# Gates of the first two chunks: from two groups of one to one group worked in parts

## The chip, the cores and the metric

The kernel runs on one core of one Trainium2 chip. The time is device microseconds of one execution; the time of a kernel is the median of its runs. Below, PE is the matrix engine (PEld its weight loads), DVE the vector engine, ACT the scalar engine, POOL the GpSimd engine and SP the SyncE queue that issues most transfers.

## What is computed

A gated linear recurrence with a complex gate, and behind it a mixer over its output. All is float32.

```python
# batch 4, heads 8, seq 768, head_dim 48
mag = sqrt(a_re**2 + a_im**2)
scale = minimum(mag, 0.999) / (mag + 1e-06)
ar, ai = a_re * scale, a_im * scale
for t in range(seq):                       # per batch and head, state is 48 x 48 complex
    S_re, S_im = ar*S_re - ai*S_im + outer(k[t], v[t]), ar*S_im + ai*S_re
    y[t] = q[t] @ S_re
x = y as (batch, seq, heads*head_dim)      # 4 x 768 x 384
u = x + (x.T @ U @ V).T                    # mixes positions through rank 32
out = u + relu(u @ w_ch1) @ w_ch2          # 384 -> 1536 -> 384
```

## The kernel before, in words

**Tiles.** The 768 positions of each of 4 batches are cut into chunks of 128, 24 chunks in all; a chunk is a tile of 128 positions by 384 (8 heads of 48). The recurrence is not run step by step. The gate of each position is written as a size and an angle, the logarithms and the angles are summed over the chunk by matmuls with triangular matrices, and q and k are weighted with exponentials and rotations made from the sums, so that what is left of a chunk is matmuls.

**Gates.** `gates(g)` (lines 531 to 653) makes these for a group of chunks (`GROUPS`, line 237). Before, the groups are chunk 0 alone, chunk 1 alone, and then pairs. `magnitudes` (547) takes a_re and a_im through Square, Ln, Exp, Relu and Sign on ACT and some additions on DVE into l, the logarithm of the size; `within` (571) sums l by one matmul ("es ps", line 575) and takes two exponentials, es. `totals` (580) has the matmuls "tot" (601), one exponential E, and transfers of E into a tile T (588). `turns` (608) takes Arctan, then the product z (DVE L611) and a scaling ("fourth", ACT), and `angles` (617) sums z by the matmul "ph" (632), to which a chunk that isn't the first of its batch adds the last row of the chunk before by "tail" (635), and rounds the sum (F, DVE L638). `waves` (641) takes Abs and two Sines into cs. The functions Ln and Exp stand in one table of ACT and Arctan and Sin in another; `switch` (322) loads a table, and the plan keeps every function that needs one between the loads that belong to it. So each group costs two loads.

**Chunks.** `prep` (661) multiplies q and k by es, then by cs into QKC, of which there is one buffer, and transposes the product on PE ("tr", line 682) into QK. `chain` (690) has the products "inner" (716) and "corners" (766), the multiplications of QK by T between them (DVE L329), and the state: "ks ps", "dk", "y".

**Mixer.** `mixer(m)` (856) works on two chunks: "mixed", "uTp", then "up" (916) with w1, Relu, then "down" with w2 (1062 for the first mixer, 1105 for others; the last mixers use fewer products, "few", 974). Its products have the lowest urgency, so they fill PE where chunks leave it free. The weights arrive as 64-bit numbers: `single` (463) loads a piece into one of two raw buffers (SP, 768 KB), converts it by six DVE operations (486 to 496), and adds a remainder by a POOL transfer (499).

**Order.** Nothing is issued in the order of the text. Each operation is given to `Plan` (45) with an engine, a cost, a rank and what it reads and writes. `order` (80) then walks through time and gives each free engine the ready operation with the smallest urgency; the urgencies are a table by kind and number (26). Where PE would stand idle before the first mixer product, the plan writes a filler: a matmul "spare" of no use (1232). After the first mixer product it writes none. The plan also reckons with the arrival of PE's program in blocks (`fetch`, 262: first 95, then every 127 records, asked for 16 ahead, 3.7 us).

The driver (1196 to 1225) says which gates are made known before which chunks:

```python
    for g in range(NG):
        load_a(g)
        magnitudes, totals, turns, waves = gates(g)
        rank = "gates", GROUPS[g][0]
        switch(rank, exps)
        ...
        magnitudes()
        if g:
            totals()
        else:
            later = [totals]
        switch(rank, trigs)
        turns()
```

## Time and profile before

| | us |
|---|---|
| median of 3 runs (704.29 to 705.83) | 705.47 |
| the profiled execution | 704.41 |
| its span, first to last instruction | 702.6 |
| PE busy / DVE busy / ACT busy / POOL busy | 681.1 / 540.1 / 418.1 / 51.8 |
| fillers on PE (line 1232), 219 of them | 61.4 |
| mean granted clock of PE | 0.990 |

The span leaves out 1.8 us around the instructions. A float32 matmul is two records on PE in most of its uses, so the 219 fillers are 438 records in the profile; transposes are one record. Busy times are sums of durations; on PE neighbouring matmuls overlap, so the pace is read from starts. In the part on costly groups, the name in front of the arrow is the tile that is written. In the answer on waits the columns are the sum, the number and the longest of the waits; "issue" means that nothing that the profile records was waited for.

The first stage goes to 152.24 us, where the first up matmul starts. In it, chunks 0 to 5 are prepared and w1 and part of w2 are converted.

### The profile page before, as it was taken

The numbers are of one execution on the slowest core, as the hardware profiler recorded it, in microseconds if no ns is written. First come the engines' busy times: TensorE is split into PE (matmuls) and PEld (weight loads), VectorE is DVE, ScalarE is ACT, GpSimd is POOL, SyncE is SP. The second block draws the span as 40 slices with busy tenths as digits, with TensorE's granted clock in tenths as the row PEclk, the third lists the DMA queues.
The fourth block names the chain that finished last, engine by engine and source line by source line (L and its number), as shares of the span: only waits on it lengthen the run. The fifth ranks groups of instructions, "written<-read, shape, count | busy, mean of one in ns | idle before, by whom it ended". The sixth has DMA issues, their size and how long they took to land.

```text
span 702.6 us, 27047 instructions
## 1 busy us (share of the span) xinstructions
PE 681.1 (97%) x12148; PEld 601.0 (86%) x12148; DVE 540.1 (77%) x877; ACT 418.1 (60%) x778; POOL 51.8 (7%) x92
## 2 busy tenths in 40 slices
PE   7989998999999999999999999999999999999998
PEld 6877877877688888879888888889999999899997
DVE  5899998888898887759678487879887787455734
ACT  6786987678797687977784953651624415041230
POOL 5110000011000010001000000000000000000000
PEclk9999999799999999999999999999999999999999
DMA  7876855498424343252334032040121000000000
GB/s 185 172 184 149 186 103 141 91 209 176 99 51 90 68 94 76 41 109 53 63 77 93 9 67 59 10 98 26 23 42 35 14 27 17 18 7 24 7 18 22
DMA packets 165267, 53.24 MB, mean 76 GB/s; under 512 B 154080, under 2 KB 160416, under 8 KB 165152
## 3 DMA queue, kind: packets, MB, share of 16 engines
q1 hardware_dynamic: 161072, 42.26, 27.7%
q0 software_dynamic: 4080, 9.27, 5.6%
q8 instruction: 95, 1.56, 0.9%
q14 instruction: 20, 0.16, 0.1%
HBM read 33.59 MB, written 4.72 MB: 55 GB/s over the span
## 4 chain that ended last, share of the span: by engine, by line
PE 79%; ACT 9%; DVE 7%; issue 3%; DMA 1%; SPq 0%; DVEq 0%; ACTq 0%
PE down L1105 21%; PE few L974 12%; PE up L916 12%; PE inner L716 6%; PE tr L682 5%; ACT gate L326 3%; PE dk L802 3%; PE y L841 3%; PE spare L1232 2%; PE ks ps L787 2%; PE down L1062 2%; PE es ps L575 2%; PE ph L632 2%; PE tot L601 2%; PE y L833 2%
## 5 line engine op out<-in xcount | busy, mean ns | idle before, releaser
L329 DVE TENSOR_TENSOR QK<-QK,T 112x1024 f32<-112x1024 f32 x120 | 145.8, 1221 | 6.5 <-PE corners L766 5.3
L916 PE MATMUL up<-uT,w 128*128 128x256 f32 x432 | 98.7, 381 | 0.0
L916 PEld LDWEIGHTS up<-uT,w 128*128 128x128 f32 x432 | 80.7, 190 | 12.0 <-DVE uT L906 0.2
L326 ACT ACTIVATE gate<-gate 128x768 f32<-128x768 f32 (+1 forms) x91 | 71.0, 792 | 6.2 <-DVE gate L611 2.0
L1105 PE MATMUL down<-w,h 128*128 128x192 f32 x396 | 73.2, 330 | 0.0
L982 ACT COPY h<-few 128x512 f32<-128x512 f32 x36 | 20.8, 584 | 85.2 <-PE few L974 85.1
L685 ACT COPY QK<-tr 112x512 f32<-112x512 f32 x96 | 52.0, 588 | 32.6 <-PE tr L682 32.3
L1105 PEld LDWEIGHTS down<-w,h 128*128 128x128 f32 x396 | 63.9, 190 | 2.7 <-issue 1.3
L1232 PE MATMUL spare<-ident 128*128 128x128 f32 x438 | 61.4, 289 | 2.1 <-POOL ident masks.py:199 1.5
L332 DVE TENSOR_TENSOR h<-few,h 128x512 f32<-128x512 f32 x54 | 37.2, 691 | 30.2 <-PE few L974 26.2
L1232 PEld LDWEIGHTS spare<-ident 128*128 128x128 f32 x438 | 55.1, 198 | 5.9 <-issue 1.9
L716 PEld LDWEIGHTS inner<-QK 112*32 112x32 f32 x4608 | 45.9, 110 | 16.4 <-issue 10.7
L716 PE MATMUL inner<-QK 112*32 112x16 f32 (+1 forms) x4608 | 51.2, 190 | 4.9 <-issue 4.5
L682 PE MATMUL tr<-ident,QKC 128*112 128x128 f32 x384 | 51.9, 275 | 1.2 <-ACT QK L685 0.8
L329 DVE TENSOR_TENSOR QKC<-qk,cs 128x768 f32<-128x768 f32 x48 | 45.9, 956 | 9.3 <-PE tr L682 6.6
L332 DVE TENSOR_TENSOR xo<-down,xo 128x192 f32<-128x192 f32 (+1 forms) x79 | 29.8, 388 | 27.0 <-PE down L1105 25.2
L682 PEld LDWEIGHTS tr<-ident,QKC 128*112 128x112 f32 x384 | 42.3, 133 | 6.1 <-ACT QK L685 1.8
L974 PE MATMUL few<-gate,w 128*128 128x128 f32 x336 | 43.1, 277 | 0.0
L1049 POOL DMA_DIRECT2D out_dram<-xo x32 | 17.9, 560 | 338.9 <-DVE xo L332 278.8
L850 ACT COPY xo<-y 64x192 f32<-64x192 f32 x96 | 30.1, 313 | 19.2 <-PE y L841 16.0
L722 DVE COPY_PREDICATED DG<-mask,inner 128x128 f32<-128x128 int32 (+1 forms) x72 | 24.6, 344 | 20.4 <-PE inner L716 20.3
L974 PEld LDWEIGHTS few<-gate,w 128*128 128x128 f32 x336 | 40.0, 192 | 0.3
(131 smaller groups left out, 1272.0 us busy)
## 6 DMA issues: line engine op xcount, KB each, us to landing
stage<-in_moe_w_ch_dram SPq DMA_DIRECT2D x12, 768.0 KB, 6.5
gate<-in_a_re_dram SPq DMA_DIRECT2D x24, 192.0 KB, 3.2
gate<-in_a_im_dram SPq DMA_DIRECT2D x24, 192.0 KB, 4.3
qk<-in_q_dram SPq DMA_DIRECT2D x24, 192.0 KB, 4.0
qk<-in_k_dram SPq DMA_DIRECT2D x24, 192.0 KB, 4.4
VP<-in_v_dram SPq DMA_DIRECT2D x24, 192.0 KB, 3.3
w<-stage POOLq DMA_DIRECT2D x12, 384.0 KB, 5.7
T<-E SPq DMA_DIRECT2D x44, 96.0 KB, 2.5
```

What stands on the lines that cost most here:

```text
L326: return nc.scalar.activation(out=o, in_=i, func=f, **kw)
L329: nc.vector.tensor_tensor(out=o, in0=a, in1=b, op=OP.mult)
L332: nc.vector.tensor_tensor(out=o, in0=a, in1=b, op=OP.add)
L682: nc.tensor.transpose(out=get(*ps)[0:DQ, j], in_=get(*qkc)[:, hh * HH + j].rearrange("p u d -> p (u d)")[:, 0:DQ], identity=ident)
L685: ACT(c_act(HH * CH) - 0.05, R1, lambda u=u, hh=hh, ps=ps: nc.scalar.copy(out=get(*QK)[:, u, hh * HH:(hh + 1) * HH], in_=get(*ps)[0:DQ]), ...
L716: nc.tensor.matmul(out=get(*ps)[js, h], lhsT=k_of(h)[:, js], rhs=part(q_of(h)[:, js], "p"), start=True, stop=True, tile_position=(0, j * BLK))
L722: nc.vector.copy_predicated(out=to, mask=part(mask[:, n], "p").unsqueeze(1).to_broadcast(list(to.shape)), data=a if hf < 8 else a.rearrang ...
L850: ACT(c_act(HH * D), RR, lambda r=r, u=u: nc.scalar.copy(out=get(*xi).rearrange("p (a u d) -> p a u d", u=2, d=D)[r * HC:(r + 1) * HC, :, ...
L916: nc.tensor.matmul(out=get(*ps)[:, e], lhsT=w1[:, f, (ff + e) * 128:(ff + e + 1) * 128], rhs=get(*uT)[:, f], start=(f == 0), stop=(f == KD ...
L974: nc.tensor.matmul(out=get(*ps)[:, q], lhsT=w()[:, q * 128:(q + 1) * 128], rhs=v[0](), start=(n == 0 and q == 0), stop=True, skip_group_ch ...
L1105: nc.tensor.matmul(out=get(*to)[:, part], lhsT=x(j), rhs=y[:, j], start=(first and j == 0), stop=(j == KH - 1), skip_group_check=not first)
L1232: nc.tensor.matmul(out=spare[0], lhsT=ident, rhs=ident, start=True, stop=True)
```

## The change

The first two chunks become one group. Within it, operations are still made for one chunk each (`PARTS`), so that chunk 0 doesn't wait for chunk 1 at every step, but both chunks stand between the same table loads: 12 groups instead of 13. `totals` of the first group isn't put off any more, and its transfers carry two chunks each. `PAIRED` and `AT_ONCE` count groups and are shifted by one, so that they mean the same chunks. The loads of a of chunks 0 and 1 are given ranks next to each other. A preparation waits for its own chunk's part of cs.

All urgencies are replaced by other numbers. This moves instructions on every engine through the whole kernel.

```diff
-    GROUPS = [(0, 1), (1, 2)] + [(n, n + GC) for n in range(2, NT, GC)]
+    GROUPS = [(n, n + GC) for n in range(0, NT, GC)]
+    PARTS = [[(n, n + 1) for n in range(GC)]] + [[g] for g in GROUPS[1:]]
...
-    PAIRED = 6
+    PAIRED = 5
...
-    AT_ONCE = (0, 1, 2, 3)
+    AT_ONCE = (0, 1, 2)
...
-                SP(c_dma(DM), ("load", (0, 0.5, 3)[g] if g < 3 else lo + 3), lambda nm=nm, src=src, i=i: nc.sync.dma_start(
+                SP(c_dma(DM), ("load", i / 20 if g == 0 else 3 if g == 1 else lo + 3), lambda nm=nm, src=src, i=i: nc.sync.dma_start(
...
         def magnitudes():
             ring(l, "GL", GL)
-            ACT(ca, R1, lambda: act(t(x), t(ar), AF.Square), [ar], [x])
+            for part in PARTS[g]:
+                magnitudes_of(*part)
+
+        def magnitudes_of(lo, hi):
+            t, R1, W = t_of(lo, hi), ("gates", lo), (hi - lo) * DM
+            ca, cd = c_act(W), c_dve(W)
+            X, Y, L, N = (b + (lo,) for b in (x, y, l, n))
+            AR, AI = ([b + (i,) for i in range(lo, hi)] for b in (ar, ai))
+            ACT(ca, R1, lambda: act(t(x), t(ar), AF.Square), AR, [X])
...
         def turns():
-
-            table(ca, R2, lambda: act(t(x), t(x), AF.Arctan), [], [x])
+            for part in PARTS[g]:
+                turns_of(*part)
...
         def waves():
-            cs = ("cs", g)
-            buffer(cs, "cs", 2, [128, GC, H, 2, D])
+            buffer(("cs", g), "cs", 2, [128, GC, H, 2, D])
+            for part in PARTS[g]:
+                waves_of(*part)
...
-                [qk, ("cs", g)], [qkc])
+                [qk] + [("cs", g, (w, part)) for w in range(2)], [qkc])
...
         magnitudes()
-        if g:
-            totals()
-        else:
-            later = [totals]
+        totals()
```

An excerpt of the urgencies:

```diff
-    "w2": {0: -111.09, 2: 522.21, 4: 896.97, 6: -52.37, 8: 604.14, 10: 640.8, 12: -317.28},
-    "gates": {0: -265.04, 1: 268.17, 2: 43.76, 4: -996.63, 6: 89.37, 8: 509.61, 10: -55.71, 12: 809.99, 14: -95.12,
-        16: 160.61, 18: -122.91, 20: -425.54, 22: -1729.17},
+    "w2": {0: -1266.56, 2: -21.8, 4: -981.82, 6: -74.99, 8: 354.48, 10: -1170.63, 12: 259.42},
+    "gates": {0: 253.11, 1: -1390.93, 2: -0.7, 4: -1280.16, 6: 565.76, 8: -1068.17, 10: -187.84, 12: -54.04, 14: 550.2,
+        16: 60.85, 18: -1317.29, 20: 219.78, 22: -1069.82},
```

More of the change, by code (lines that the diff above doesn't have):

```diff
@@ L26 @@
 URGENCY = {
-    "w1": {0: 577.09, 1: -1319.32, 2: 484.43, 3: -236.69, 4: 471.82, 5: -1058.73, 6: 187.51},
-    "w2": {0: -111.09, 2: 522.21, 4: 896.97, 6: -52.37, 8: 604.14, 10: 640.8, 12: -317.28},
-    "gates": {0: -265.04, 1: 268.17, 2: 43.76, 4: -996.63, 6: 89.37, 8: 509.61, 10: -55.71, 12: 809.99, 14: -95.12,
-        16: 160.61, 18: -122.91, 20: -425.54, 22: -1729.17},
-    "angles": {0: -126.72, 1: -84.17, 2: -1567.87, 4: -1150.68, 6: -325.13, 8: 105.31, 10: 61.73, 12: 732.88,
-        14: -1148.2, 16: 655.25, 18: 538.84, 20: -116.45, 22: 233.15},
@@ L33 @@
-    "prep": {0: -1639.87, 1: -367.99, 2: -1022.47, 3: -12.47, 4: -106.92, 5: -436, 6: -74.87, 7: 260.1, 8: -1682.29,
-        9: 278.7, 10: 47.08, 11: 569.46, 12: -1452.21, 13: -249.3, 14: -287.97, 15: -363.52, 16: -269.7,
-        17: -1664.43, 18: -240.93, 19: 153, 20: -1089.48, 21: -198.95, 22: -127.5, 23: 757.32},
-    "levels": {0: 731.75, 1: -318.03, 2: 17.02, 3: -430.68, 4: -436.08, 5: -170.38, 6: 221.56, 7: 124.72, 8: -1567.59,
-        9: -1453.16, 10: -1698.36, 11: -60.78, 12: 502.58, 13: 523.21, 14: -1475.59, 15: 515.81, 16: -1265.88,
-        17: 487.77, 18: -263.92, 19: 16.81, 20: 723.89, 21: -1759.83, 22: -1111.46, 23: -160.12},
@@ L39 @@
-    "rest": {0: 468.93, 1: -1086.12, 2: 24.25, 3: -218.54, 4: -1119.41, 5: -346.92, 6: 0.68, 7: -1700.8, 8: 681.55,
-        9: -376.72, 10: -229.72, 11: -305.85, 12: -1069.62, 13: 601.71, 14: -282.72, 15: 204.95, 16: 59.77,
-        17: 552.08, 18: -62.45, 19: 466.03, 20: -1105.96, 21: -351.77, 22: -1688.33, 23: 463.92},
+    "w1": {0: -1281.04, 1: -1220.88, 2: -1207.45, 3: 315.61, 4: 369.7, 5: 444.04, 6: 70.95},
+    "w2": {0: -1266.56, 2: -21.8, 4: -981.82, 6: -74.99, 8: 354.48, 10: -1170.63, 12: 259.42},
@@ new lines @@
+    "gates": {0: 253.11, 1: -1390.93, 2: -0.7, 4: -1280.16, 6: 565.76, 8: -1068.17, 10: -187.84, 12: -54.04, 14: 550.2,
+        16: 60.85, 18: -1317.29, 20: 219.78, 22: -1069.82},
+    "angles": {0: -1303.82, 1: -1298.68, 2: -1227.51, 4: 58.46, 6: 57.41, 8: -1315.3, 10: -1053.02, 12: 620.73,
+        14: 187.25, 16: -891.55, 18: 148.92, 20: -161.38, 22: -1298.55},
+    "prep": {0: -1294.88, 1: 125.6, 2: -26.13, 3: 96.73, 4: 102.92, 5: 146.86, 6: 553.65, 7: 283.9, 8: 120.02,
+        9: -991.17, 10: -32.91, 11: 113.94, 12: -202.96, 13: 14.8, 14: 318.58, 15: 357.43, 16: 269.94, 17: 521.08,
+        18: 158.53, 19: -163.04, 20: 127.47, 21: 184.1, 22: 205.57, 23: -1204.94},
@@ new lines @@
+    "levels": {0: 201.22, 1: 294.56, 2: -15.94, 3: 207.38, 4: -1236.01, 5: 275.3, 6: 572.46, 7: 14.34, 8: -1057.92,
+        9: 306.71, 10: 125.53, 11: 133.52, 12: 287.15, 13: 373.35, 14: 82.96, 15: 592.16, 16: 289.79,
+        17: -1204.78, 18: -1075.08, 19: 91.86, 20: 733.17, 21: -1309.23, 22: 119.93, 23: -1230.17},
+    "rest": {0: 93.55, 1: 47.27, 2: 273.41, 3: 257.67, 4: -1050.04, 5: -1068.08, 6: -1240.77, 7: -1208.87, 8: -1033.73,
+        9: -1290.81, 10: 34.85, 11: -1143.56, 12: -162.29, 13: -197.24, 14: -1046.5, 15: 612.4, 16: 244.97,
+        17: -1261.21, 18: 98.64, 19: -1031.75, 20: -1297.46, 21: 239.78, 22: 384.61, 23: 164.23},
@@ L531, in gates @@
     def gates(g):
-        lo, hi = GROUPS[g]
-        W = (hi - lo) * DM
-        R1, R2 = ("gates", lo), ("angles", lo)
-        ca, cd = c_act(W), c_dve(W)
         x, y, l, n, z, ar, ai = names = [(nm, g) for nm in ("x", "y", "l", "n", "z", "ar", "ai")]
-        def t(b):
-            a = get(*b)
-            return (a.rearrange("p c h d -> p (c h d)") if b[0][0] == "a" else a)[:, 0:W]
+        first = GROUPS[g][0]
         def of(b, i):
-            return get(*b)[:, (i - lo) * DM:(i - lo + 1) * DM]
+            return get(*b)[:, (i - first) * DM:(i - first + 1) * DM]
@@ L547, in magnitudes, with t_of, t @@
+        def t_of(lo, hi):
+            def t(b):
+                a = get(*b)
+                return (a.rearrange("p c h d -> p (c h d)") if b[0][0] == "a" else a)[:, (lo - first) * DM:(hi - first) * DM]
+            return t
         def magnitudes():
             ring(l, "GL", GL)
-            ACT(ca, R1, lambda: act(t(x), t(ar), AF.Square), [ar], [x])
-            ACT(ca, R1, lambda: act(t(y), t(ai), AF.Square), [ai], [y])
-            DVE(cd, R1, lambda: add(t(x), t(x), t(y)), [y], [x])
-            DVE(c_one(W), R1, lambda: nc.vector.tensor_scalar(out=t(x), in0=t(x), scalar1=M2LO, scalar2=M2HI, op0=OP.max,
-                                                              op1=OP.min), [], [x])
@@ L554, in magnitudes @@
-            ACT(ca, R1, lambda: act(t(n), t(ar), AF.Abs), [ar], [n])
-            table(ca, R1, lambda: act(t(l), t(x), AF.Ln), [x], [l])
-            table(ca, R1, lambda: act(t(x), t(l), AF.Exp, scale=0.5), [l], [x])
-            DVE(cd, R1, lambda: add(t(x), t(x), t(n)), [n], [x])
-            table(ca, R1, lambda: act(t(y), t(l), AF.Exp, scale=-0.5, bias=leps), [l], [y])
-            table(ca, R1, lambda: act(t(y), t(y), AF.Ln, bias=1.0), [], [y])
-            ACT(ca, R1, lambda: act(t(l), t(l), AF.Relu, scale=-0.5, bias=lmax), [], [l])
@@ L562, in magnitudes @@
-            DVE(cd, R1, lambda: nc.vector.scalar_tensor_tensor(out=t(l), in0=t(l), scalar=LNMAX, in1=t(y), op0=OP.subtract,
-                                                               op1=OP.add), [y], [l])
-            table(ca, R1, lambda: act(t(x), t(x), AF.Ln), [], [x])
-            table(ca, R1, lambda: act(t(x), t(x), AF.Exp, scale=-1.0), [], [x])
-            DVE(cd, R1, lambda: mul(t(x), t(x), t(ai)), [ai], [x])
-            ACT(ca, R1, lambda: act(t(n), t(ar), AF.Sign, bias=tiny), [ar], [n])
+            for part in PARTS[g]:
+                magnitudes_of(*part)
@@ new lines, in magnitudes_of @@
+        def magnitudes_of(lo, hi):
[4 more added lines that the diff above has]
+            ACT(ca, R1, lambda: act(t(x), t(ar), AF.Square), AR, [X])
+            ACT(ca, R1, lambda: act(t(y), t(ai), AF.Square), AI, [Y])
+            DVE(cd, R1, lambda: add(t(x), t(x), t(y)), [Y], [X])
+            DVE(c_one(W), R1, lambda: nc.vector.tensor_scalar(out=t(x), in0=t(x), scalar1=M2LO, scalar2=M2HI, op0=OP.max,
+                                                              op1=OP.min), [], [X])
+            ACT(ca, R1, lambda: act(t(n), t(ar), AF.Abs), AR, [N])
+            table(ca, R1, lambda: act(t(l), t(x), AF.Ln), [X], [L])
+            table(ca, R1, lambda: act(t(x), t(l), AF.Exp, scale=0.5), [L], [X])
+            DVE(cd, R1, lambda: add(t(x), t(x), t(n)), [N], [X])
+            table(ca, R1, lambda: act(t(y), t(l), AF.Exp, scale=-0.5, bias=leps), [L], [Y])
+            table(ca, R1, lambda: act(t(y), t(y), AF.Ln, bias=1.0), [], [Y])
+            ACT(ca, R1, lambda: act(t(l), t(l), AF.Relu, scale=-0.5, bias=lmax), [], [L])
+            DVE(cd, R1, lambda: nc.vector.scalar_tensor_tensor(out=t(l), in0=t(l), scalar=LNMAX, in1=t(y), op0=OP.subtract,
+                                                               op1=OP.add), [Y], [L])
+            table(ca, R1, lambda: act(t(x), t(x), AF.Ln), [], [X])
+            table(ca, R1, lambda: act(t(x), t(x), AF.Exp, scale=-1.0), [], [X])
+            DVE(cd, R1, lambda: mul(t(x), t(x), t(ai)), AI, [X])
+            ACT(ca, R1, lambda: act(t(n), t(ar), AF.Sign, bias=tiny), AR, [N])
@@ L568, in magnitudes, with within @@
             for i in range(lo, hi):
-                within(i)
-        def within(i):
+                within(i, R1, L)
+        def within(i, R1, L):
             ps, es = ("es ps", i), ("es", i)
@@ L575, in within @@
             PE(0.65, R1, lambda: nc.tensor.matmul(out=get(*ps), lhsT=mid, rhs=of(l, i), start=True, stop=True),
-               [l, ("mid", 0)], [ps, ("sums", g, i)], takes=[es], steps=2)
+               [L, ("mid", 0)], [ps, ("sums", g, i)], takes=[es], steps=2)
             for u in range(2):
@@ L583, in totals @@
             ring(tt, "T", TS)
-            for i in range(lo, hi):
-                of_blocks(i)
+            lo, hi = GROUPS[g]
+            for part in PARTS[g]:
+                for i in range(*part):
+                    of_blocks(i, ("gates", part[0]))
             for u in range(2):
@@ L590, in totals, with of_blocks @@
                         in_=get(*e)[w * 64:w * 64 + D, 0:hi - lo].rearrange("p c h b -> p c (h b)")), [e], [tt + ((u, w),)])
-        def of_blocks(i):
+        def of_blocks(i, R1):
+            lo = first
             ps, e = ("tot", i), ("E", g)
@@ L608, in turns, with turns_of, angles @@
         def turns():
-            table(ca, R2, lambda: act(t(x), t(x), AF.Arctan), [], [x])
+            for part in PARTS[g]:
+                turns_of(*part)
+        def turns_of(lo, hi):
+            t, R2, W = t_of(lo, hi), ("angles", lo), (hi - lo) * DM
+            ca, cd = c_act(W), c_dve(W)
+            X, N, Z = x + (lo,), n + (lo,), [z + (i,) for i in range(lo, hi)]
+            table(ca, R2, lambda: act(t(x), t(x), AF.Arctan), [], [X])
             DVE(cd, R2, lambda: nc.vector.scalar_tensor_tensor(out=t(z), in0=t(x), scalar=math.pi / 4, in1=t(n),
-                                                               op0=OP.subtract, op1=OP.mult), [x, n], [z])
-            ACT(ca, R2, lambda: act(t(z), t(z), AF.Identity, scale=1.0 / math.pi, bias=fourth), [], [z])
+                                                               op0=OP.subtract, op1=OP.mult), [X, N], Z)
+            ACT(ca, R2, lambda: act(t(z), t(z), AF.Identity, scale=1.0 / math.pi, bias=fourth), [], Z)
             for i in range(lo, hi):
-                angles(i)
-        def angles(i):
+                angles(i, R2)
+        def angles(i, R2):
             fo = lambda i: F[:, i % GC]
@@ L623, in angles @@
             zi = z + (i,)
-            first = i < NCH
-            if where(i)[1] > 0 and not first:
+            whole = i < NCH
+            if where(i)[1] > 0 and not whole:
                 POOL(1.0, R2, lambda: nc.gpsimd.dma_start(out=of(z, i)[0:1], in_=fo(i - 1)[CH - 1:CH], accum_op=OP.add),
@@ L629, in angles @@
             psum(ps, "T", [128, DM], [128, 512])
-            carry = first and i > 0
+            carry = whole and i > 0
             PE(0.65, R2, lambda: nc.tensor.matmul(out=get(*ps), lhsT=prefix, rhs=of(z, i), start=True, stop=not carry),
@@ L641, in waves, with waves_of @@
         def waves():
-            cs = ("cs", g)
-            buffer(cs, "cs", 2, [128, GC, H, 2, D])
-            def half(u):
-                return get(*cs).rearrange("p c h u d -> p (c h) u d")[:, 0:W // D, u]
-            fs = [("F", i) for i in range(lo, hi)]
-            ft = heads(F.rearrange("p c m -> p (c m)")[:, lo % GC * DM:lo % GC * DM + W])
-            ACT(ca, R2, lambda: act(half(0), ft, AF.Abs), fs, [cs + (0,)])
-            table(ca, R2, lambda: act(half(1), ft, AF.Sin, scale=2.0 * math.pi), fs, [cs + (1,)])
-            table(ca, R2, lambda: act(half(0), half(0), AF.Sin, scale=-2.0 * math.pi, bias=quarter), [], [cs + (0,)])
+            buffer(("cs", g), "cs", 2, [128, GC, H, 2, D])
+            for part in PARTS[g]:
+                waves_of(*part)
+        def waves_of(lo, hi):
+            cs, R2, ca = ("cs", g), ("angles", lo), c_act((hi - lo) * DM)
+            def half(u):
+                return get(*cs).rearrange("p c h u d -> p (c h) u d")[:, (lo - first) * H:(hi - first) * H, u]
+            fs, c0, c1 = [("F", i) for i in range(lo, hi)], cs + ((0, lo),), cs + ((1, lo),)
+            ft = heads(F.rearrange("p c m -> p (c m)")[:, lo % GC * DM:lo % GC * DM + (hi - lo) * DM])
+            ACT(ca, R2, lambda: act(half(0), ft, AF.Abs), fs, [c0])
+            table(ca, R2, lambda: act(half(1), ft, AF.Sin, scale=2.0 * math.pi), fs, [c1])
+            table(ca, R2, lambda: act(half(0), half(0), AF.Sin, scale=-2.0 * math.pi, bias=quarter), [], [c0])
         return magnitudes, totals, turns, waves
@@ L664, in prep @@
         qk, QK = ("qk", i), ("QK", i)
+        part = next(p[0] for p in PARTS[g] if p[0] <= i < p[1])
         buffer(QK, "QK", 3, [DQ, 2, H, CH])
```

## The prediction

> **What bounds the kernel now.** I read the page first: busy shares, then the rows of slices.

> ```profile
> PE 681.1 (97%) x12148; PEld 601.0 (86%) x12148; DVE 540.1 (77%) x877; ACT 418.1 (60%) x778; POOL 51.8 (7%) x92
> ...
> PE   7989998999999999999999999999999999999998
> ...
> PEclk9999999799999999999999999999999999999999
> ```

> PE is busy everywhere. In the start part of that is fillers: the matmuls of line 1232 that the plan writes where it finds PE without work. They stand in the program, so if PE is late it runs them all the same, and its lateness goes to the end. Then busy times by stage:

> ```profile
> 27.00:60.00 33.00, 29.86 (x626) 25.55 (x627) 32.00 (x46) 24.89 (x44) 2.85 (x3) 1.00 0.72 172
> 60.00:90.00 30.00, 28.52 (x672) 24.20 (x671) 28.58 (x42) 24.27 (x43) 1.72 (x2) 1.00 0.76 158
> 90.00:115.00 25.00, 23.46 (x643) 19.77 (x642) 24.80 (x38) 21.77 (x43) 1.72 (x2) 1.00 0.62 137
> 115.00:131.00 16.00, 12.58 (x312) 10.38 (x312) 11.87 (x16) 7.92 (x18) 0.00 (x0) 0.68 0.36 94
> 131.00:152.00 21.00, 20.73 (x455) 16.94 (x454) 18.66 (x30) 14.89 (x30) 2.89 (x3) 1.00 0.67 137
> 152.00:400.00 248.00, 246.30 (x4469) 207.16 (x4468) 196.65 (x285) 195.72 (x344) 18.04 (x25) 1.00 0.40 84
> ```

> The columns are PE, PEld, DVE, ACT, POOL, granted clock, DMA share, GB/s. Up to 115 us DVE is full (32.00 of 33, 28.58 of 30, 24.80 of 25) and PE's time holds all the fillers; the first up matmul is at 152.24, and from there PE is 99% busy with work. So the end is: PE's real work, the same in both kernels (6,179 matmuls), plus fillers, plus what PE waits or runs slowly. I then asked what PE waited for before 152 us:

> ```profile
> PE es ps L575 <- DVE mask L440: 3.6, 1, 3.6
> PE inner L716 <- issue: 3.4, 2, 3.1
> ```

> The first is the very start: the first chunk's gates are ready at 11.13, its 20 fillers end at 7.57. The second stands in PE's order of time at

> ```profile
> 115.47 0.54 PE L716 MATMUL inner<-QK 112*32 112x32 f32 x34
> 119.11 0.45 PE L716 MATMUL inner<-QK 112*32 112x32 f32 x30 [3.10 <-issue]
> ```

> It is no data wait: it falls in the middle of a product. Counting matmul records from the start, PE's waits named issue are at records 731, 1749, 2001, 2128 and 2382, each within 3 of 95 + 127k, so PE waits there for a block of its program. The DMA part lists 95 packets of 1.56 MB for instructions, 16 KB each. The SyncE queue shows what was in the way of this one:

> ```profile
> 107.89 0.73 SPq L456 DMA_DIRECT2D qk<-in_k_dram  x1
> 109.28 0.88 SPq L477 DMA_DIRECT2D stage<-in_moe_w_ch_dram  x2
> ```

> Two weight loads of 768 KB were issued together behind q and k; the DMA share is 0.86 to 1.04 from 108 to 116 us. Then the clock:

> ```profile
> 116.00:119.00 3.00, 0.00 (x1) 0.00 (x0) 1.43 (x2) 2.83 (x4) 0.00 (x0) 1.00 0.49 136
> 119.00:122.00 3.00, 2.89 (x108) 2.47 (x111) 2.15 (x4) 0.00 (x0) 0.00 (x0) 0.74 0.02 5
> 122.00:125.00 3.00, 3.00 (x91) 2.85 (x88) 3.00 (x4) 1.23 (x5) 0.00 (x0) 0.50 0.21 36
> 125.00:128.00 3.00, 2.68 (x76) 2.14 (x75) 1.71 (x4) 1.06 (x4) 0.00 (x0) 0.50 0.27 72
> 128.00:131.00 3.00, 3.00 (x13) 2.15 (x12) 2.58 (x3) 1.81 (x4) 0.00 (x0) 0.55 0.58 141
> 131.00:134.00 3.00, 3.00 (x158) 2.73 (x157) 1.51 (x3) 1.40 (x4) 0.00 (x0) 1.00 0.98 194
> ```

> After the wait the granted clock is 0.50 for 10.24 us (120.44 to 130.68 in the clock's records).

> [...] The row shows three slow windows: matmuls that take 5.7 us at their mean pace elsewhere (y L833 0.68 us there against 1.27 here, es ps 0.91 against 1.65) filled 10.24 us, 0.3 of it waiting, so 4.3 us were lost. [...] The block cost 3.1 + 4.3 = 7.4 us, and nothing took it up: from 119 to 152 PE waits only 0.32.

> **The change part by part.**

> Work removed: one pair of table loads (26 to 24 loads) and 4 SyncE issues (8 of 48 KB become 4 of 96 KB). A load takes 1.28 on ACT and the next activation starts 1.29 after its start (13.59 to 14.88). [...] ACT isn't on the path that sets the end; the value shows up only in the fillers, so I don't add it again. The gate operations keep their 384-element form (0.52 us): splitting adds none.

> Fillers: the program order of PE has 219 before and 203 after, all ahead of the first up matmul; the real work ahead of that matmul is nearly equal (71.4 and 70.7 us at the trace's mean paces). A filler at full clock takes 3.74/16 = 0.234 (16 fillers at 46.30). 16 x 0.234 = 3.7 us less. All of it counts: PE's queue is what ends last.

> The start, by hand. New ACT order up to the first rotation: Ln of chunk 0 still at 7.7 (it waits for DVE's clamp, unmoved), and chunk 1's squares lie in the wait ahead of it. By relu of chunk 0 three operations of chunk 1 were inserted, one of them in a 0.1 hole: relu moves from 9.70 to 10.3, es ps from 11.1 to 11.6. Chunk 1's relu follows 5 starts later, es ps at 14.05. Then 2 exponentials, sign, 2 x 2 es, E twice: table load at 19.1 instead of 13.6. Arctan, z and fourth for two chunks: ph at 22.2 (17.33 before); from ph to the first tr 4.6 us as in the trace, plus 0.4 for the second chunk's steps: 27.2 against 21.95. So PE's first chunk work comes 5.25 later. But by then PE has done 15 more fillers (66 against 51: 3.5) and 2.8 more real work (es ps, tot, ph and tail of chunk 1), 6.3 in all. That is 1.0 us better than the count alone, since the wait of 3.6 shrinks to about 1.7 with 30 fillers, and the half clock from 11.21 to 14.63 that it brought (1.5 us) should not come; against it stand new waits at ph and tr of about 1 us each. I take -1.0 (bounds -2.5 and +0.8).

> Loads moved: a of chunk 1 is issued second pair, ahead of prefix, first w1 piece, mask, q, k and v of chunk 0. 384 KB at the 275 GB/s of 4 to 8 us is 1.4 us. prefix feeds POOL's mid, which stood behind memsets until 7.32; its totals end at 10.2 and are asked for at 16.9. q and k feed DVE at 14.45 before and at about 19 now. Both are covered; uncovered it would be the 1.4. T from E now leaves for both chunks at 19.1 instead of 22.6 and 33.2.

> The rest of the order: the urgencies reorder every engine. The waits for DVE and ACT from 25 to 115 us sum to 4.7; I see no reason for another sum and take 0 (bounds -2 and +4).

> Block waits: at mean paces, the time from 143 records ahead of a block boundary to it was 3.2, 3.7, 2.7 and 2.4 us at records 2000, 2127, 2254 and 2381; after it is 2.9 at 857, 3.05 at 2000 and 3.6 at 2254. So blocks are asked for less tightly where before was tightest, and the w2 loads are no longer issued in twos (each stands alone in SyncE's order, later; a pair of w1 loads stays near 30 us, among fillers). One new short wait (near 0.8, like the row of 0.72) against four small ones of 1.9 in all: even. The 7.4 goes if no large load stands ahead of a tight block, stays if one does. I take -7.4 (bounds -7.4 and 0).

> Sum: -3.7 - 1.0 - 7.4 = -12.1. The span of 702.6 becomes 690.5; its execution took 704.41, so 692.3 for such an execution. The median shown is 705.47, 1.06 above: 693.4.

> **The rivals.**

> The block wait recurs. For it: T, AT, q and k transfers still fill the DMA queues, and 2000 is tight. Against it: no pair of weight loads. Only the plan's gain stays: -4.7, 700.8.

> The gain is eaten by new waits (DVE at 98% from 27 to 115 us, a plan that counts nothing unplanned): 705.

> Slower: late w2. Before, three of six w2 pieces are converted ahead of the first up; after, one. The plan writes no fillers once mixer products begin, so a hole there is not seen in my count. Before, the last piece is issued at 172.51, lands 5.7 later at 178.2, and is asked for after 182.0. After, by hand, from the first up: five conversions of 4.15 us on DVE with gates between, the last held behind a QKC multiply that waits for tr; it ends at 31.4, lands near 38, and is asked for at 40. Slack 2, was 4. If it is late, PE stands, and if it stands near 3 us the clock halves, 4.3 more. It decides from a lateness of about 8 us (12.1 less 4.3), which loads slowed for all five pieces (6.5 each to land) could give: 712 with 15.

> **How the numbers follow.** Block wait gone 0.47 (own range 689 to 698); recurs 0.28 (697 to 703); eaten 0.05; slower 0.20. The likeliest gives 693.4. The range 687.5 to 706 takes in the first three and leaves out the slower one and a little below. A difference under 0.2% (1.4 us) can't be told from none: faster 0.75, same 0.05, slower 0.20.

> **What would show it.** Right: first up near 140 us instead of 152.24; no wait named issue over 1.5 us before it; granted clock 1.00 from 8 us on; es ps with under 2 us of wait; PE 99% from the first up. Wrong: a clock of 0.50 anywhere behind 15 us, a wait of down for the w copies, or first tr behind 29 us.

## The result, and the profile after

The changed kernel takes 694.97 us (median of 4 runs, 694.18 to 698.57), before 705.65 beside it (704.29 to 708.86): ratio 0.9863, 95% interval 0.9815 to 0.9912, in which two more executions of 700.56 and 695.59 are counted. The prediction was 693.4. In a second set of runs it took 699.05 (10 runs, 694.71 to 710.1) against 705.78, ratio 0.9898 (0.9867 to 0.9929). The 710.1, and 715.61 of after_phase below, are slow runs, over 1.5% above the fastest of the same kernel, and no ratio counts them. So the gain is 7 to 11 us, and it differs from execution to execution; the experiments show a part of why. The profiled execution is the slowest of the first four, 698.57 with a span of 696.8.

The page of the changed kernel, busy shares and granted clock in 40 slices:

```profile
PE 673.7 (97%) x12116; PEld 594.2 (85%) x12116; DVE 538.9 (77%) x877; ACT 416.5 (60%) x776; POOL 51.8 (7%) x92
...
PEclk9999999999999999999999999999999999999999
```

The 7 in before's row of the clock is gone: in the trace the clock is 1.00 from 6.7 us to 525.5. The first up matmul starts at 140.81 (152.24 before; 140 was predicted). Busy times by stage up to there (PE, PEld, DVE, ACT, POOL, granted clock, DMA share, GB/s), first before, then after:

```profile
60.00:115.00 55.00, 51.98 (x1313) 43.97 (x1312) 53.38 (x79) 46.05 (x85) 3.44 (x4) 1.00 0.69 149
115.00:152.20 37.20, 33.51 (x765) 27.45 (x765) 30.53 (x46) 23.01 (x47) 2.89 (x3) 0.86 0.54 119
```

```profile
60.00:115.00 55.00, 49.50 (x1444) 42.46 (x1443) 53.82 (x80) 39.56 (x79) 2.65 (x4) 1.00 0.58 116
115.00:140.80 25.80, 25.09 (x518) 19.97 (x509) 22.74 (x34) 22.12 (x42) 1.62 (x2) 1.00 0.69 172
```

Read DVE, the third pair. By 115 us both kernels have done as much DVE work (48.13 + 53.38 and 48.20 + 53.82; the first 60 us are not shown). Counted by DVE's work, the whole gain, 11.4 us, lies between 115 us and the first up: DVE has 7.8 less to do there, and stands idle 3.1 instead of 6.7. By tiles, summed from the start to the first up, the new order puts 5.6 of w2 conversion (about 1.3 pieces), 1.6 of gates and 0.6 of rounding behind the first up. Counted by PE's records the changed kernel is ahead already at 115 us: 518 records are left against 765, of them about 60 of fillers in both. So the rows say where the time went, but not which engine's work set it.

What PE waited for up to 140.81, in sum, number and longest:

```profile
PE inner L739 <- issue: 5.2, 5, 1.7
...
PE corners L789 <- issue: 1.2, 1, 1.2
PE es ps L583 <- DVE GL L570: 0.9, 1, 0.9
```

The 3.1 us wait has no successor of its size, but waits named issue sum to 7.0 (with two smaller rows), where before had 5.0. They still stand within a few records of 95 + 127k. The transfers show more directly that they are waits for the program: in all 14 traces 122 waits named issue are over 0.3 us, 119 of them at such a place, and in each of the 119 PE goes on 2.1 to 3.2 us after a packet of 16 KB with instructions starts. Before's wait of 3.1 us is such a case: the point 143 records ahead (127 + 16, the figures of the plan's `fetch`) passed at 111.7, the packet started at 116.78, and PE went on at 119.11.

The span is only 5.8 shorter, so 5.6 were given back behind the first up. Stage and place:

```profile
400.00:697.00 297.00, 289.75 (x4710) 270.62 (x4708) 202.87 (x375) 102.00 (x216) 12.65 (x23) 0.99 0.13 30
```

```profile
522.32 1.24 PE L739 MATMUL inner<-QK 112*32 112x16 f32 x124
525.85 0.30 PE L739 MATMUL inner<-QK 112*32 112x16 f32 x4 [2.30 <-issue]
```

Again a product is cut by a wait for nothing recorded, at record 10004 (95 + 127 x 78 is 10001), and the clock is at 0.50 from 525.5 to 528.9. Issue waits of inner behind the first up sum to 4.1, before to 1.0: 3.1 of the 5.6; the half clock is worth up to 1.7 (an estimate, half of its 3.41 us), and 0.7 is work that now stands behind the first up.

### The profile page after: what moved, and what is told of

It is laid out like the page before. It is cut to its first block, busy times and chain, and to the rows that moved or that the text cites. A ratio compares the mean times of both kernels' runs of the same rounds, so it can differ in the third digit from the quotient of the medians.

```text
span 696.8 us, 26972 instructions
## 1 busy us (share of the span) xinstructions
PE 673.7 (97%) x12116; PEld 594.2 (85%) x12116; DVE 538.9 (77%) x877; ACT 416.5 (60%) x776; POOL 51.8 (7%) x92
## 3 DMA queue, kind: packets, MB, share of 16 engines
q8 instruction: 95, 1.56, 0.9%
## 4 chain that ended last, share of the span: by engine, by line
PE 75%; ACT 10%; DVE 9%; issue 3%; DMA 2%; SPq 0%; DVEq 0%; ACTq 0%
PE down L1128 20%; PE few L997 12%; PE up L939 10%; PE tr L705 6%; PE inner L739 5%; ACT gate L327 4%; PE y L864 3%; PE dk L825 3%; DVE QK L330 2%; PE ks ps L810 2%; PE ph L650 2%; PE es ps L583 2%; PE tot L612 2%; PE y L856 2%; PE spare L1252 1%
## 5 line engine op out<-in xcount | busy, mean ns | idle before, releaser
L330 DVE TENSOR_TENSOR QK<-QK,T 112x1024 f32<-112x1024 f32 x120 | 145.4, 1217 | 7.6 <-PE corners L789 4.0
L739 PE MATMUL inner<-QK 112*32 112x16 f32 (+1 forms) x4608 | 51.3, 190 | 10.4 <-issue 9.3
L1252 PE MATMUL spare<-ident 128*128 128x128 f32 x406 | 57.8, 289 | 1.7 <-POOL ident masks.py:199 1.5
L705 PE MATMUL tr<-ident,QKC 128*112 128x128 f32 x384 | 54.2, 276 | 2.8 <-ACT QK L708 1.1
L1252 PEld LDWEIGHTS spare<-ident 128*128 128x128 f32 x406 | 52.0, 200 | 5.5 <-POOL ident masks.py:199 1.5
L1128 PE MATMUL down<-stage 128*128 128x192 f32 x198 | 36.8, 329 | 0.1
```

The costliest lines, as they stand in the source:

```text
L330: nc.vector.tensor_tensor(out=o, in0=a, in1=b, op=OP.mult)
L705: nc.tensor.transpose(out=get(*ps)[0:DQ, j], in_=get(*qkc)[:, hh * HH + j].rearrange("p u d -> p (u d)")[:, 0:DQ], identity=ident)
L739: nc.tensor.matmul(out=get(*ps)[js, h], lhsT=k_of(h)[:, js], rhs=part(q_of(h)[:, js], "p"), start=True, stop=True, tile_position=(0, j * BLK))
L1128: nc.tensor.matmul(out=get(*to)[:, part], lhsT=x(j), rhs=y[:, j], start=(first and j == 0), stop=(j == KH - 1), skip_group_check=not first)
L1252: nc.tensor.matmul(out=spare[0], lhsT=ident, rhs=ident, start=True, stop=True)
```

## The experiments

All medians stand beside runs of before on the same chip; the ratio is to those. Below, a trace is "late" at a record by as much as that record starts later than in the other trace.

| run | us | ratio, 95% |
|---|---|---|
| before_split | 703.66 | 0.9984 (0.9961 to 1.0007) |
| after_phase | 710.60 | 1.0064 (1.0032 to 1.0096) |
| after_thin4 | 698.23 | 0.9915 (0.9883 to 0.9947) |
| after_tables | 700.68 | 0.9943 (0.9919 to 0.9968) |
| after_again | 699.05 | 0.9898 (0.9867 to 0.9929) |
| after_dve8 | 704.21 | 0.9986 (0.9960 to 1.0012) |
| before_leave | 706.21 | 0.9999 (0.9977 to 1.0022) |
| after_oldurg | 731.94 | 1.0389 (1.0343 to 1.0434) |
| after_load | 700.81 | 0.9918 (0.9887 to 0.9948) |
| after_swap | 696.69 | 0.9880 (0.9851 to 0.9909) |
| before_newurg | 747.56 | 1.0593 (1.0544 to 1.0642) |
| before_both | 710.27 | 1.0051 (1.0027 to 1.0075) |

**Is it the pair of w2 loads?** before_split takes the pair apart in before's order.

```diff
     todo = plan.order()
+    todo.remove(at["load", 8.1][0])
+    todo.insert(todo.index(at["place", 4][3]) + 1, at["load", 8.1][0])
```

> Before's kernel with one transfer moved on SyncE's queue: the second of the two 768 KB w2 pieces that left together at 109.28 leaves behind the four AT transfers (122.19 in before). Theory (the pair delays the block of PE's program): the 3.10 us wait at record 2128 falls below 0.5 and the clock's 0.50 from 120.4 to 130.7 does not come; 7.4 us less, some 698 against 705.5. Rival (the block is late anyway, q and k and one piece stand before it): the wait stays above 2 us, 705 to 706. Rival (the moved piece is then late for its conversion on DVE at 140): the first up matmul does not come earlier than 150.

PE in order of time around the place (start, us, operation, the wait ahead of it):

```profile
114.36 0.43 PE L802 MATMUL dk<-VP,ks 64*48 64x48 f32 x13 [1.11 <-issue]
...
118.20 0.45 PE L716 MATMUL inner<-QK 112*32 112x32 f32 x30 [0.40 <-issue]
...
122.19 0.32 PE L833 MATMUL y<-VP,AT 64*64 64x48 f32 x5 [1.23 <-issue]
```

The wait at record 2128 fell from 3.10 to 0.40, so the pair did cause most of it. The packet that ends it starts 3.1 us after the point 143 records ahead; in the three traces that keep the pair (before, before_leave, before_both) it is 4.8 to 5.1, with waits of 2.3 to 3.1. But two neighbours grew (0.3 to 1.11 at 2001, which before_leave has too, with the pair in place; 1.23 at 2255, where before waited less than 0.2), the clock still was 0.50 for 6.8 us (122.8 to 129.6), and the first up came at 152.02. The moved piece isn't late for its conversion, but ACT waits 1.9 us for a load of a, 0.3 in before. The time is 1.1 less, an interval that holds zero. The first theory fails: of 7.4 us, at most 2.8 (the end of the interval) hang on the pair.

**The pair put into the changed kernel.** after_load.

```diff
+            if pieces == 2:
+                for u in range(2):
+                    nc.sync.dma_start(out=copy[u], in_=moe_w_ch2[u * 256:(u + 1) * 256].rearrange("(c p) m -> c p m", p=128).bitcast(U32))
```

> The changed kernel with two more transfers of 768 KB on SyncE's queue (two w2 pieces copied into memory that nothing reads), directly behind q and k at 99.84: what before had at 109.28, put in front of the tight blocks at records 2000 and 2127. Theory of the prediction (such a pair delays a block by 3 to 4 us and the clock then drops for three windows): a wait of 2.5 us or more at record 1999 or 2126 (0.5 and 0.95 without it), granted clock 0.50 for 7 to 10 us behind it, first up 5 to 8 later than 140.7, the time 704 to 707 (699 for the changed kernel beside the last runs). Rival (a pair alone is not enough, or what it takes is hidden behind DVE, which is full there): first up within 2, the time 698 to 701.

```profile
112.00 0.68 PE L739 MATMUL inner<-QK 112*32 112x16 f32 x58 [2.15 <-issue]
```

```profile
113.00:120.00 7.00, 7.00 (x173) 6.75 (x167) 5.43 (x8) 2.27 (x8) 0.85 (x1) 0.54 0.51 100
```

The wait at 2126 is 2.15 us, the clock 0.50 for 6.8 us, the first up 3.3 later. In the time (700.81) that isn't told from the changed kernel, and it lies where the rival had it. Each falls short of what the theory said; and after_swap, below, shows the same half clock with no pair at all.

**Does the place of the blocks matter?** after_phase moves every block by 64 records with 32 matmuls of 32x32 (`small`), together about 2 us long (an estimate: 64 records of 32 ns, as before_both shows them at clock 1.00).

```diff
+        if n < 0 and fillers == 1:
+            for _ in range(32):
+                small()
```

> The changed kernel with 32 matmuls of 32x32 behind the first filler: 64 matmul records, so that every block of PE's program begins 64 records earlier in the work; the work itself costs some 1 us where PE waited 0.9. Theory (a block wait is a matter of where a block falls: asked for 143 records ahead, there about 3.7 us later, and 128 records of inner pass in 1.3 us): worked out over the record times of the changed kernel, the block waits grow from 1.4 to 10.5 us in all, or from 4.0 to 15.6 if a block takes 4.2; 9 to 12 us slower, and a few more where a wait of 2 us or more halves the clock: 704 to 710. Rival (block waits come from transfers in the way, not from the place): within 1.5 us of the changed kernel, 694 to 696.5.

Its waits of PE over the span:

```profile
PE inner L739 <- issue: 9.3, 6, 2.6
PE dk L825 <- issue: 4.5, 2, 3.0
PE y L864 <- issue: 2.9, 2, 1.7
...
PE tot L612 <- issue: 1.2, 1, 1.2
```

710.60: by the ratios 12 to 14 us slower than the changed kernel. The block waits sum to 18.2 (10.7 in the changed kernel's trace, counting those over 0.3), the clock is halved in four stretches of together 17.1 us ahead of the first up, which starts at 154.09; 2.3 of that is a later first tr. So a shift by half a block undoes the whole change. From the record times alone 704 to 710 had been expected, with a block 3.7 us after the point 143 records ahead; the 3.7 is the plan's figure and no run shows it: where PE waited, it went on 3.1 to 10.4 us after that point. That the waits grow with nothing added to the transfers speaks for the theory; the later first tr, about 2 us, isn't part of it.

**Does a filler cost its length?** after_thin4.

```diff
+        thin = n < 0 and fillers > 66 and fillers % 4 == 0
+        (small if thin else plan.ops[n][4] if n >= 0 else idle)()
```

> The changed kernel with every fourth filler behind the first 66 (34 of 137) shrunk to a matmul of 32x32, so that the count of records and the place of the blocks stay. Theory (PE's order is what ends last, so fillers count in full): 34 x about 0.21 = 7.2 us less, 688. Rival (DVE is full from 27 to 115 us, the filler only covers its lateness): waits of PE for DVE grow by as much, 693 to 696. In between, each shrunk filler gives back what its stage lets it.

```profile
60.00:90.00 30.00, 28.40 (x755) 23.44 (x745) 29.90 (x44) 26.21 (x52) 1.71 (x2) 1.00 0.68 140
...
115.00:122.00 7.00, 7.00 (x119) 6.24 (x112) 4.16 (x5) 2.70 (x7) 0.86 (x1) 0.52 0.63 131
```

Nothing was gained: record 2200 starts at 111.78, in the changed kernel at 111.62. But the edit did not take time out of PE's order. A shrunk filler between full ones made its stretch longer: the four records from the one ahead of it to the one behind it take 592 ns, in the changed kernel 447, at all 13 such places ahead of record 2200. (A run of shrunk ones alone is short: 32 ns a record in before_both at clock 1.00, where a full filler has 112.) And the waits of PE for DVE and ACT, which the rival wanted to see grow, are 2.1 us from 26.2 to 112, against 2.4. So this run decides neither for the theory nor for the rival; that DVE is 29.90 of 30 busy fits the rival, no more. Then the clock fell to 0.50 from 115.2 to 122.0, behind three block waits of 0.78, 0.95 and 1.38, and by record 2400 it was 3.4 late. It doesn't take shrunk fillers to bring that: after_swap, below, has the same half clock with all of them in full.

**Is a table load off the path?** after_tables.

```diff
+        for nm in ((trigs, exps) if rank[1] == 0 and name == trigs else ()) + (name,):
+            nc.scalar.preload_act_table_set(nm)
```

> The changed kernel with two more activation table loads in front of the first arctan (at 18.35), which is one pair, as much as the change saved. By the prediction (loads on ACT are not on the path): 694 to 696. Rival (at the start PE waits for ACT's chain, and its fixed order hands lateness on to the end): 2 x 1.28 = 2.6 us more, 697.5, and 1.7 to 4 more where the longer wait at ph halves the clock, up to 701.

ACT in order of time, then PE's waits up to its first up:

```profile
18.34 3.86 ACT L326 ACT_TABLE_LOAD   x3
22.21 0.94 ACT L330 ACTIVATE gate<-gate 128x384 f32<-128x384 f32 x2
```

```profile
PE ph L653 <- ACT gate L330: 3.3, 2, 3.0
```

Three loads take 3.86, 1.29 each, and the arctan follows at once. PE's wait at ph grows by 2.5 and record 200 is 3.14 late, with one half-clock window (24.5 to 27.9). It is still 2.56 late at record 2100; the first up is 1.8 late, because block waits near 114 were shorter this time. The ratio is 0.0045 (3.2 us) above after_again's, with intervals that overlap by 0.001. So at the start ACT is on the path, and a pair of loads there costs about its length; how much of it is the half-clock window isn't told apart.

**The changed kernel again**, after_again, with no edit.

> The changed kernel as it is, beside the runs below on their chip. 693 to 697 in most executions. If the 2.3 us block wait at 525 with its half clock is a chance of one execution, this trace lacks it and its span is near 693; if it belongs to the order of the work, it is there again.

PE behind the first up:

```profile
PE inner L739 <- issue: 4.6, 4, 2.5
```

The wait at 10004 is there again (2.55), with 3.4 us of half clock, and the time is above the 693 to 697 that were expected. Of the six traces with this order and no edit near it (two unedited, after_thin4, after_tables, after_dve8, after_load) five have it: it belongs to the order, though few transfers stand there (DMA share 0.10 from 520 to 540). The delay lies ahead of the transfer: the packet starts 3.5 to 3.9 us behind record 9858 in the five, 0.9 in after_tables, where PE doesn't wait. Why it starts so late stays open.

**DVE work ahead of the first up.** after_dve8 adds some to the changed kernel.

```diff
+        if n >= 0 and plan.ops[n][0] == "DVE" and plan.ops[n][3] == ("w2", 0) and seen < 4:
+            seen += 1
+            mul(scratch, scratch, scratch)
+            mul(scratch, scratch, scratch)
```

> The changed kernel with eight VectorE multiplications of 128x768 (0.95 us each, 7.6 in all, on a buffer that nothing uses yet) among the first four steps of the w2 conversion at 127.8 to 130.7: about the DVE work of the two w2 pieces that before converts ahead of its first up matmul and the changed kernel behind it. Theory D (up to the first up matmul DVE's work sets the pace, and the change gained by taking 8.3 us of conversions out of it): first up 5.5 to 7.6 later, 146 to 148.5 instead of 140.8, and the time 701 to 703. Theory P of the prediction (PE's own order with its fillers sets it): first up at most 2 later, the time 694 to 697.

```profile
133.00:146.00 13.00, 11.29 (x127) 8.61 (x120) 12.90 (x20) 8.51 (x13) 0.85 (x1) 0.88 0.41 104
```

The first up comes at 145.81, 5.2 later than in after_again, and the time is 5.2 more. DVE is now full (12.90 of 13). One half-clock window (132.6 to 136.0) is worth up to 1.7 of it. Theory D was a little high for the first up, and the time lies above its 701 to 703; theory P (2 at most) fails.

**DVE work taken out of before**, before_leave.

```diff
+        if kind in (("w2", 2), ("w2", 4)) and plan.ops[n][0] in ("DVE", "POOL"):
+            if kind not in skipped:
+                skipped.add(kind)
+                nc.gpsimd.memset(w2[:, kind[1]:kind[1] + 2], 0.0)
+            continue
```

> Before's kernel without the conversion of the two w2 pieces that stands ahead of the first up matmul (136 to 147): their 12 DVE operations (8.3 us) and two accumulating transfers are left out, and two POOL memsets put zeros there, so part of the mixers' second product is zero. Theory D: the first up comes 4 to 8.3 earlier than 152.2, and the time is 697 to 701. Theory P: PE is 20.73 of 21 us busy from 131 to 152 with its own order, so the first up moves by less than 1.5 and the time stays at 704 to 706.

```profile
140.00:152.00 12.00, 12.00 (x196) 9.42 (x192) 4.02 (x7) 8.96 (x17) 0.78 (x1) 1.00 0.66 142
```

DVE has little to do (4.02 of 12), and nothing is gained: PE is 12.00 of 12 busy with its own order. The first up of this trace is at 154.50, but it was 2.7 late already at record 1984, with a half clock from 43.6 to 50.5 that the edit doesn't touch; from that record to the first up it takes 40.0 us, before 40.5. Here theory P holds, with a limit: the order, with its 33 fillers in this stretch, was made for a DVE that still had the conversions to do. In the same trace the block wait at 2128 is 2.32, and the clock 0.50 from 122.1 to 132.4.

**Both taken out of before**, before_both: the last 26 fillers shrunk as well.

```diff
+        (small if n < 0 and fillers > 193 else plan.ops[n][4] if n >= 0 else idle)()
```

> The same as the earlier kernel without the two conversions of w2 pieces (their DVE operations and transfers left out, zeros put there, so part of the mixers' second product is zero), and besides the last 26 fillers ahead of the first up matmul, from 131 us on, shrunk to matmuls of 32x32 that keep the count of records. Leaving out the conversions alone moved the first up by -0.4 against record 1984, and left the time at 706. Theory (two bounds side by side: DVE's work and PE's fixed order with its fillers; only both together give anything): the stretch from record 1984 to the first up is 3 to 5.5 us shorter than the 40.0 of that run, the time 701 to 703. Rival (a third chain, through ACT and the latencies between engines, holds that stretch): shorter by less than 1.5, the time 705 to 706; or PE with fewer fillers falls to half clock behind 140, and it is longer.

```profile
131.00:140.00 9.00, 7.82 (x282) 6.75 (x278) 7.14 (x10) 6.48 (x16) 0.00 (x0) 0.87 0.53 105
140.00:148.00 8.00, 8.00 (x121) 6.01 (x122) 1.11 (x2) 4.64 (x9) 0.78 (x1) 0.50 0.80 159
```

It is worse by 4 us. Here the shrunk fillers stand together and are short, and the clock fell to 0.50 from 137.6 to 151.3 and once more from 154.7 to 158.1, and the same stretch takes 45.6 instead of 40.0. In before_leave, with full fillers, the clock is 1.00 from 140 to 152. This is the second branch of the rival. What both would give at full clock this run can't say.

**The grouping without its order, and the order without its grouping.** after_oldurg is the changed kernel with before's table of urgencies, before_newurg the reverse.

> The changed kernel with before's table of urgencies: the grouping and the operations of one chunk alone, planned by the old numbers. Its PE order has 268 fillers, 65 more than the changed kernel and 49 more than before. If the grouping itself brings the gain, it is near 695; if the gain is the new order (what is put ahead of the first up), it is slower than before: by the fillers 49 x 0.234 = 11.5 us more than 705, some 716; between, 700 to 706, if fillers only cover waits.

> Before's kernel with the changed kernel's table of urgencies: groups and operations as before, ordered by the new numbers. Its PE order has 280 fillers. If the table alone brought the gain, it is below 700; if each table fits only its own grouping, as with the old table on the new grouping (732), it is at 715 or more.

They take 731.94 and 747.56 us; the first up is at 174.3 and 171.9, with 268 and 280 fillers, and DVE is busy only 140.4 and 145.4 us of those. 731.94 is worse than any of the three cases that had been expected. Each table fits its own grouping alone. The named edit under the old numbers costs 26 us; with its own it gains.

**The wait at 10004 taken away**, after_swap: two few products (16 records) ahead of the inner group.

```diff
+    for n in few:
+        todo.remove(n)
+        todo.insert(todo.index(levels), n)
```

> The changed kernel with two few products (4 matmuls each) put ahead of the 64 inner matmuls at 522.5, behind which PE waited 2.3 to 2.55 us for its block at record 10004 in four of the six traces of kernels with this order, with 3.4 us at half clock after it. The 128 records of inner pass in 1.3 us; 16 records later they no longer fill the window in which the block comes. Theory: that wait falls below 0.6 and the half clock at 526 is gone, 2 + 1.7 us less: 695 to 697 where the changed kernel had 699, ratio to before 0.984 to 0.987 against 0.990. Rival (the wait moves to the next block, or DVE is held by the later inner): ratio 0.989 to 0.992.

```profile
527.31 1.27 PE L739 MATMUL inner<-QK 112*32 112x16 f32 x128
```

```profile
113.00:120.00 7.00, 6.72 (x145) 6.46 (x144) 5.65 (x8) 2.28 (x8) 0.85 (x1) 0.52 0.63 119
```

The group is no longer cut, and no half clock follows: against after_again this trace is 2.98 late at record 9600 and 0.41 at 10200, 2.6 us gained. It was late because of 113 to 120 us, a part that the edit doesn't touch: two block waits of 1.28 and 1.33, then 6.8 us at half clock, which the two traces of the unedited kernel do not have. 696.69 is the best median of this later series; the ratio, 0.988, lies between the theory's 0.984 to 0.987 and the rival's 0.989 to 0.992, and its interval overlaps the changed kernel's. So the wait is gone in the trace, and the gain in time isn't shown.

## Why the prediction was right, point by point

The number was right, and the first up came within 1 us of its place. Of the steps, only the number of fillers and the half clock had their size. That the median came within 1.6 us is in part luck: for an execution like the profiled one the prediction said 692.3, and that took 698.57; the second set of runs lies 5.6 above the prediction.

| step | predicted | measured |
|---|---|---|
| fillers | -3.7 | 61.4 to 57.8 busy: -3.6 |
| start | -1.0 | first tr 26.24 (27.2 predicted), 66 fillers ahead of it as predicted: about -2.0 by the same count |
| 3.1 us block wait and small ones | -3.1 | issue waits 5.0 to 7.0: +2.0 |
| half clock at 120 to 131 | -4.3 | none ahead of the first up: -4.3 |
| PE's waits for DVE and ACT, 25 to 115 us | 0 | 4.8 to 2.4: -2.4 |
| behind the first up | 0 | +5.6 in the profiled execution |

Up to the first up the measured column sums to -10.3, and the first up came 11.4 earlier; an estimated 0.7 of the rest is work that now stands behind it.

Of the five signs of being right that the prediction named, two came in: first up near 140, and es ps with under 2 us of wait. Three did not: one wait named issue is 1.73 us, PE is less than 99% busy behind the first up, and the clock is 0.50 from 525.5 to 528.9, which it had also named as a sign of being wrong.

**Fillers.** "All of it counts: PE's queue is what ends last" isn't shown. As bookkeeping PE's queue does hold 3.6 us less. Whether that is a cause, or whether the fillers lie in the time of DVE, which is 29.90 of 30 us busy from 60 to 90 in that run, after_thin4 can't say, since its shrunk fillers took no time out. after_dve8 speaks against PE's queue alone: 7.6 us more on DVE moved the end by 5.2.

**Start.** The order worked out by hand held: es ps waited 0.9 (1.7 predicted), ph and the first tr 0.5 and 0.4 (about 1 each), and the half clock of 11 to 15 us is gone as said. "ACT isn't on the path that sets the end" is wrong at the start: after_tables handed the length of two loads, 2.56 us, on to record 2100. The load itself took 1.28 in before and 1.29 in after_tables (three in a row 3.86), and two more lengthened PE's wait at ph by 2.5.

**Block waits.** "The 7.4 goes if no large load stands ahead of a tight block" named one cause of several. The pair made most of the 3.1 us wait (before_split, after_load). But whether a block is late depends as much on where it falls (after_phase: half a block further, 12 to 14 us), and half clock followed two or three waits of about 1 us within 10 us too (after_thin4, after_swap, before_split), though not always: the changed kernel's own trace has 0.73, 0.95 and 1.10 there and stays at 1.00. That the small ones would be "even" was wrong by 5 us ahead of the first up (1.9 before, 7.0 after) and by 3 behind it, where the prediction took PE's 99% for granted; it is 97.6% from 400 us on.

**Half clock.** Predicted and measured agree for the traces of the unedited changed kernel, which have none ahead of the first up. All four traces with before's order have 6.8 to 10.2 us of it near 120 to 132. But the new order isn't free of it: after_swap, unedited up to there, has 6.8 us. That is some 3 us (an estimate, half of the 6.8) in some executions and not in others. With the wait at 10004 it may be a good part of the spread from 694 to 702: the executions of 694.18, 694.71 and 694.75 us have a mean clock of 0.999 to 1.000, those of 700.17 and 702.34 us 0.995 and 0.993; but one of 698.89 has 1.000 too, so it isn't all of it.

**What the prediction left out** is DVE: 7.8 us of its work moved behind the first up, where it is 74% busy (211.12 us of 259 from 141 to 400, 202.87 of 297 from there). It matters in the new order (after_dve8: 7.6 more make 5.2) and not in the old one (before_leave: 0.4), where PE's fixed order ends as late. In the new order lateness of PE stays as well (after_thin4: 3.4 at record 2400, 3.2 at the first up). The reading that fits is that two bounds stood side by side, and that the plan moved both. It isn't shown: removing both from before should then give the 11 us, and the one attempt lost the clock. How the 11 us divide between DVE's work, PE's order and the half clock stays open.

**The rivals.** The block wait recurs in part, as smaller waits and at 10004. Late w2 did not come: no wait of down for w is in the trace, and no price of moving the conversions is seen. That the grouping by itself brings the gain is refuted by after_oldurg, 731.94.

## What to carry to other kernels

Where two engines are both nearly full, price a change on each of them, stage by stage, and take the later; here an edit that relieved one gave nothing (before_leave, ratio 0.9999), and edits that burdened one cost most of their length (after_dve8: 5.2 of 7.6 us; after_tables: 2.56 us at record 2100 of two loads of 1.29). Before a filler is taken for a cost, ask whose time it lies in, and what the clock does without it (before_both: 0.50 from 137.6 to 151.3); and look in the trace whether the edit that should shorten it did (after_thin4). In a kernel of many short matmuls count records, since a shift of the program by half a block can be worth as much as the change that is studied (after_phase: 12 to 14 us).
